# Pooled attention, expert layer and slot experts on one core: the last quarter of w2 reordered early, second-layer sums per column half, and the last token rows written by pairs

## The chip, the cores and the metric

The kernel is one program on one core of a Trainium2 chip. The core has a matrix engine (PE, whose weight loads stand apart as PEld), a vector engine (DVE), a scalar engine (ACT), GpSimd (POOL) and a sync engine (SP). SP issues every DMA of this kernel; 16 DMA engines carry them out. The metric is the device time of one execution in microseconds. The engines run their own instructions in order and wait for each other through semaphores.

## The reference

Three stages follow each other, on 4608 tokens (36 tiles of 128) and 512 columns, all in float32:

```
k_p, v_p = mean of k, v over 8 neighbouring positions
x   = softmax(q k_p^T / sqrt(64)) v_p          # 8 batches x 8 heads, as 4608 x 512
x   = relu(x @ w_in)^2 @ w_out                 # 512 -> 2048 -> 512
logits = x @ phi                               # 4608 x 32 slots
d   = softmax of logits over the tokens;  slot_input = d^T @ x       # 32 slots x 512
slot_out[e] = relu(slot_input[e] @ w1[e]) @ w2[e]     # 8 experts, 4 slots each, 512 -> 1024 -> 512
c   = softmax of logits over the 32 slots
out = c @ slot_out                             # 4608 x 512
```

The change touches only the end of this: the product with w2 (8 x 1024 x 512, 16.8 MB), the last line, and when a quarter of w2 is read.

## The kernel before, in words

Up to about 680 us a table of slots (`ev`, filled by `at`, run by `run_slot`) drives a loop over token tiles: attention of a tile, its product with w_in (L492, the bulk of the matrix work), squares, logits, and running sums over the tokens. The squared tiles `g` go to DRAM (`g_dram`, L532) and come back turned. The keys and values (`kv`, L147) and the queries (`qt`, L130, in 16 or more small pieces) are loaded through SP between these stores. A scheduler places the instructions; SP works through its DMAs in order, over eight semaphores, so that a DMA is issued only after the one eight places before it has landed.

Then comes the tail. `project` makes the slot inputs. `first(r, n, kks)` is the first expert layer for experts 4r to 4r+3 and half n of the hidden columns, four experts side by side in 32 columns of the PE array each; `turn_h` turns its result. Between `turn_h(0, 1)` and `first(1, 1)` five transposes (`slot_turn`, L783) turn the slot weights c of the token groups 4 to 8 (a group is four token tiles), and `slot_out` copies them back.

`second` (through `queued`, so its instructions have line L1228) adds one chunk of 128 hidden rows of the second layer. The kernel before first sums all eight chunks of experts 0 to 3 and the first four chunks (fc 0 to 3) of experts 4 to 7, 512 columns wide, into one PSUM bank `misc`; ACT copies it to `slot_part`. `slots_of(h)` then does one half h of the columns: the last four chunks (fc 4 to 7) of experts 4 to 7 at 256 columns into `po`, DVE adds `slot_part` (L1295), PE spreads the sum over the four 32-row groups (`pr`, L1297), ACT copies it to `slots` (L1298). The weights for these last chunks are read by `load_w2(h, 1, 1)`, eight DMAs of 512 KB (L872) in runs of 256 columns, 1 KB.

`combine(h, ss, n)` makes the output of the token groups 2n and 2n+1 for one half of the columns: eight matmuls with 32 rows (one 32-row group of the array for each u) and 128 columns, then two copies on DVE and two on ACT, and four stores of 256 KB in 1 KB runs (L1325). It runs for h = 0, then `slots_of(1)`, then for h = 1. `combine_rows(g)` does the groups 4 to 8 over all 512 columns: four matmuls of 32 rows by 128 columns (L1334) into four banks, four copies, four stores of 256 KB, 2 KB a row (L1345). The matmul results lie in six PSUM banks (`l1`, `gT`, `att`, two each); `l`, `gT` and `att` in the rows below are these.

Of the kernel before, what the change touches and what calls it, by code (L numbers as in the profile page):

```python
# [17 lines left out]
def kernel(  # L18
# [21 lines left out]
    P = 128  # L40
# [44 lines left out]
    wo_dram = dram.tile([P, DFF // P, DM], F32, tag="wo_dram", name="wo_dram")  # L85
    g_dram = [dram.tile([2, NQ, CPQ, P, P], F32, tag=f"g_dram{t}", name=f"g_dram{t}") for t in range(0, NT - 4, 2)]
# [767 lines left out]
    def load_w2(h, r, fg):  # L854
# [15 lines left out]
        for i in range(4):  # L870
            fc = 4 * fg + i
            w2t["last"] = nc.sync.dma_start(  # L872
                out=parts[i],
                in_=w2[4 * r:4 * r + 4, fc * P:(fc + 1) * P, h * HD:(h + 1) * HD].rearrange("e p d -> p e d"),
            )
            w2t[h, r, fc] = [parts[i][:, j] for j in range(4)]

# [96 lines left out]
    for j in range(PC, NQ):  # L974
        for kk in range(KD):
            at(CS[j - 2][kk], paced, conv_in, j, kk)
    at(0, load_w, "in", 2)
# [290 lines left out]
    queued(slot_turn, 4, 8)  # L1268
    behind(["siT"], slot_out, 4, 8, nc.vector.tensor_copy)
    queued(slot_turn, 8, 9)  # L1270
    slot_out(8, 9, nc.scalar.copy)
# [17 lines left out]
    def slots_of(h):  # L1289
        po = ps1.tile([P, HD], F32, tag="pl", name="po")  # L1290
        for fc in range(NFC // 2, NFC):
            second(po, NR - 1, fc, w2t[h, NR - 1, fc], fc == NFC // 2, fc == NFC - 1)
        so = slot_part[:, h]
        ss = slots[:, h]
        nc.vector.tensor_tensor(out=so, in0=po, in1=so, op=ALU.add)  # L1295
        pr = ps1.tile([P, HD], F32, tag="pl", name="pr")
        mark[f"pr{h}"] = nc.tensor.matmul(pr, s4rep.rearrange("p a b -> p (a b)"), so)  # L1297
        nc.scalar.copy(out=ss, in_=pr)  # L1298
        return ss
# [3 lines left out]
    def combine(h, ss, n):  # L1303
# [6 lines left out]
        for a, g in enumerate(groups):  # L1310
            for u in range(4):
                b = slice(32 * u, 32 * u + 32)
                with ExitStack() as es:
                    if (a, u) != (0, 0):
                        es.enter_context(tc.issue_after(mark["row"].ins))
                    mark["row"] = nc.tensor.matmul(banks[u][:, a * HD:(a + 1) * HD], lt_sb[b, 4 * g:4 * g + 4].rearrange("p u s -> p (u s)"), ss[b])
# [10 lines left out]
    def combine_rows(g):  # L1327
        banks = []
        for u in range(4):
            banks.append(ps(tags[n_out[0] % 3]))  # L1330
            n_out[0] += 1
        for u in range(4):
            b = slice(32 * u, 32 * u + 32)
            mark["row"] = nc.tensor.matmul(  # L1334
                banks[u],
                lt_sb[b, 4 * g:4 * g + 4].rearrange("p u s -> p (u s)"),
                slots[b].rearrange("p h d -> p (h d)"),
            )
        for u in range(4):
            o = gp.tile([P, DM], F32, tag="g", name="o")  # L1340
            if u % 2:
                nc.scalar.copy(out=o, in_=banks[u])
            else:
                nc.vector.tensor_copy(o, banks[u])
            nc.sync.dma_start(out=out[(4 * g + u) * P:(4 * g + u + 1) * P], in_=o)  # L1345

    po = psm()
    chunks = [(0, fc) for fc in range(NFC)] + [(NR - 1, fc) for fc in range(NFC // 2)]
    for r, fc in chunks:
        if (r, fc) == (0, NFC // 2):  # L1350
            turn_h(1, 0)
            turn_h(1, 1)
        second(po, r, fc, w2t[r, fc], (r, fc) == chunks[0], (r, fc) == chunks[-1])
    slot_part = p2.tile([P, 2, HD], F32, tag="r", name="slot_part")
    nc.scalar.copy(out=slot_part.rearrange("p h d -> p (h d)"), in_=po)
    ss0 = slots_of(0)
    with tc.issue_after(w2t["last"].ins):
        for n in range(2):
            combine(0, ss0, n)
    ss1 = behind(["row"], slots_of, 1)  # L1360
    for n in range(2):
        combine(1, ss1, n)
    for g in range(4, NT // 4):
# [31 lines left out]
```

## Time and profile before

| | us |
|---|---|
| three runs, median (lowest to highest) | 754.03 (751.69 to 756.07) |
| the profiled execution | 751.86 |
| its span in the trace | 750.1 |
| PE busy in the span | 715.6 |
| DVE busy | 524.3 |
| ACT busy | 387.8 |

The profiled execution lasted 1.8 us longer than its span, and it was 2.2 us faster than the median of the runs. Times in the rows below are microseconds from the start of the span. A matmul in float32 stands as two instructions in the trace, so that 16 matmuls of the program are "x32" there. A busy PE is one that has a matmul in flight, which says nothing on how well the array is filled.

### The profile page before, as it was taken

To read this page: it belongs to the slowest core of one execution; us is meant where nothing else is said; L and a number is where in the kernel's file an instruction comes from. 1 tells how busy PE (TensorE), PEld (TensorE's weight loads), DVE (VectorE), ACT (ScalarE), POOL (GpSimd) and SP (SyncE) were. 2 spreads that over 40 slices of the span, in tenths; PEclk is the share of its full clock that TensorE was granted. 3 is DMA by queue.
4 is the path that set the end of the run, shared out by engine and by line. 5 is a ranking of instruction groups with operands and counts; after the bars stand their busy time and mean duration, and the time that the engine had idled before them with its cause. 6 is when DMAs were issued, how large, how long until landed. Compare 5 with 4: busy or idle time off the path is not lost.

```text
span 750.1 us, 13911 instructions
## 1 busy us (share of the span) xinstructions
PE 715.6 (95%) x4969; PEld 497.4 (66%) x4969; DVE 524.3 (70%) x1048; ACT 387.8 (52%) x1132; POOL 136.5 (18%) x151
## 2 busy tenths in 40 slices
PE   7799899999999999999999999999999999999985
PEld 7677678787776767666666656667666766764342
DVE  4998854497896788878979787778878574414132
ACT  3766767464656456346646462637466453333132
POOL 2234400004971400050342120320000000000000
PEclk9999999999999999999999999999999999999996
DMA  8967945658776996686998788879676434988998
GB/s 256 257 198 237 260 136 155 218 144 258 213 224 163 274 258 185 191 251 169 250 283 232 195 242 241 229 204 262 181 231 213 141 127 147 410 326 341 394 303 337
DMA packets 213012, 175.05 MB, mean 233 GB/s; under 512 B 75216, under 2 KB 169424, under 8 KB 212944
## 3 DMA queue, kind: packets, MB, share of 16 engines
q1 hardware_dynamic: 212944, 174.17, 75.7%
q8 instruction: 39, 0.64, 0.3%
q14 instruction: 29, 0.24, 0.1%
HBM read 126.94 MB, written 47.19 MB: 232 GB/s over the span
## 4 chain that ended last, share of the span: by engine, by line
PE 56%; DVE 19%; DMA 9%; ACT 6%; issue 5%; POOL 3%; SPq 1%; POOLq 0%; DVEq 0%; ACTq 0%
PE l L492 33%; PE misc L743 3%; ACT es L258 2%; DMA kv<-in_v_dram 2%; POOL w L429 2%; PE pl L616 2%; ACT aT L306 2%; DVE es L287 2%; DVE aT L308 2%; PE l L1228 2%; PE att L340 2%; DMA kv<-in_k_dram 2%; PE gT L340 2%; DMA tmp<-g_dram 1%; PE misc L1228 1%
## 5 line engine op out<-in xcount | busy, mean ns | idle before, releaser
L492 PE MATMUL l<-w,xh 128*128 128x512 f32 x1152 | 380.0, 409 | 4.4 <-DVE tmp L528 1.6
L492 PEld LDWEIGHTS l<-w,xh 128*128 128x128 f32 x1152 | 207.8, 189 | 70.3 <-issue 16.9
L492 PE MATMUL l<-w,xl 128*128 128x512 f32 x576 | 229.5, 400 | 0.3 <-DVE xl L351 0.3
L520 ACT ACTIVATE r<-l 128x512 f32<-128x512 f32 x142 | 85.6, 604 | 153.4 <-PE l L492 145.4
L492 PEld LDWEIGHTS l<-w,xl 128*128 128x128 f32 x576 | 108.4, 188 | 29.5 <-issue 4.2
L154 POOL TENSOR_TENSOR kv<-kv 72x512 f32<-72x512 f32 x40 | 53.9, 1350 | 221.5 <-DMA kv<-in_v_dram 115.2
L306 ACT COPY aT<-turned 32x256 f32<-32x256 f32 (+1 forms) x168 | 67.8, 404 | 25.5 <-DVE turned L328 22.7
L258 ACT ACTIVATE es<-att,mx 128x72 f32<-128x72 f32 x120 | 37.1, 336 | 24.1 <-DVE mx L253 23.7
L528 DVE TENSOR_TENSOR g<-l,r 128x512 f32<-128x512 f32 x55 | 37.5, 682 | 17.0 <-ACT r L520 10.8
L580 DVE STREAM_TRANSPOSE turned<-turned 128x1024 f32<-128x1024 f32 x39 | 47.5, 1229 | 1.9 <-DMA turned<-g_dram 1.8
L258 ACT ACTIVATE es<-gT,mx 128x72 f32<-128x72 f32 x120 | 36.7, 330 | 9.8 <-DVE mx L253 9.8
L308 DVE COPY aT<-turned 32x256 f32<-32x256 f32 (+1 forms) x120 | 40.5, 337 | 1.7
L429 POOL TENSOR_TENSOR w<-tmp,w 128x512 fp32r<-128x512 f32 x16 | 28.4, 1780 | 61.9 <-ACT w L427 53.2
L530 ACT ACTIVATE g<-r 128x512 f32<-128x512 f32 x54 | 34.4, 639 | 0.7
L528 DVE TENSOR_TENSOR tmp<-l,r 128x512 f32<-128x512 f32 x33 | 22.6, 684 | 17.1 <-ACT r L520 14.4
L287 DVE TENSOR_TENSOR es<-es,rs 128x576 f32<-128x576 f32 x36 | 33.3, 927 | 0.9
L580 DVE STREAM_TRANSPOSE tmp<-tmp 128x1024 f32<-128x1024 f32 x25 | 30.3, 1224 | 5.2 <-DMA tmp<-g_dram 5.2
L155 POOL TENSOR_TENSOR kv<-kv 72x256 f32<-72x256 f32 x40 | 33.6, 848 | 0.9
L374 ACT ACTIVATE tmp<-st 128x512 f32<-128x512 f32 x32 | 21.5, 676 | 14.9 <-DMA st<-in_moe_w_in_dram 10.0
L376 DVE TENSOR_SCALAR tmp<-tmp 128x512 uint32<-128x512 uint32 x32 | 15.5, 485 | 16.3 <-ACT tmp L374 16.3
L743 PE MATMUL misc<-g,d 128*32 128x512 f32 x134 | 25.7, 629 | 1.2 <-DVE d L730 0.7
L385 DVE SCALAR_TENSOR_TENSOR tmp<-st,tmp 128x512 f32<-128x512 uint32 x32 | 26.3, 824 | 0.6
(232 smaller groups left out, 1060.2 us busy)
## 6 DMA issues: line engine op xcount, KB each, us to landing
g_dram<-g SPq DMA_DIRECT2D x95, 256.0 KB
w<-in_moe_w_dram SPq DMA_DIRECT2D x44, 512.0 KB
turned<-g_dram SPq DMA_DIRECT2D x39, 512.0 KB
tmp<-g_dram SPq DMA_DIRECT2D x25, 512.0 KB
g_back<-g_dram SPq DMA_DIRECT2D x40, 256.0 KB
kv<-in_k_dram SPq DMA_DIRECT2D x32, 288.0 KB
kv<-in_v_dram SPq DMA_DIRECT2D x32, 288.0 KB
out_dram<-o SPq DMA_DIRECT2D x36, 256.0 KB
```

The lines of the kernel that those rows point to most:

```text
L154: eng.tensor_tensor(out=x[:, :, 0:4], in0=x[:, :, 0:4], in1=x[:, :, 4:8], op=ALU.add)
L258: mark["es", t] = nc.scalar.activation(out=es[:, e], in_=sv[:, h], func=AF.Exp, bias=mx[:, e:e + 1], accum_out=rsum[:, t % 8, e, 0:1],)
L287: mark["norm", t] = nc.vector.tensor_tensor(out=es, in0=es, in1=rs.unsqueeze(2).to_broadcast([P, H, SP]), op=ALU.mult)
L306: nc.scalar.copy(out=dst, in_=src)
L308: eng[e].tensor_copy(dst, src)
L429: nc.gpsimd.tensor_tensor(out=w[kk][:, 1], in0=c, in1=w[kk][:, 0].bitcast(F32), op=ALU.subtract)
L492: mm = mark["l1", t, j] = nc.tensor.matmul(hp, steps[i][0], steps[i][1], start=(i == 0), stop=(i == n - 1))
L520: nc.scalar.activation(out=r, in_=hp, func=AF.Relu, scale=1.0 / (R * R if sq == "V" else R))
L528: mark["sq"] = nc.vector.tensor_tensor(out=dst, in0=pre, in1=src, op=ALU.mult)
L530: nc.scalar.activation(out=dst, in_=src, func=AF.Square)
L580: nc.vector.transpose(out=gc.rearrange("p (n i) -> p n i", i=32), in_=gc.rearrange("p (n f) -> p n f", f=32))
L743: mark["dg"] = nc.tensor.matmul(dp[32 * j:32 * j + 32], d[:, u], g if t < NT - 4 else natural(g), start=(u == 0), stop=(u == width(t) - 1),)
```

## The change

1. A DRAM tile `w2h` is added. Sixteen new DMAs (`split_w2`) copy the last quarter of w2 (experts 4 to 7, fc 4 to 7, 4.2 MB) from its place in w2 into `w2h`, DRAM to DRAM, in 1 KB runs; they are placed at the slots 29, 31, ... 59, each right after the latest store of `g`. The late loads of these weights then read `w2h`, where a partition's 1024 numbers (four experts, 256 columns) lie together: 4 KB runs.
2. The 512-wide sum in `misc` now ends with experts 0 to 3. Experts 4 to 7 are summed per column half over all eight chunks (`half_of`), fc 0 to 3 from 256-column slices of the same tiles. The second half's chunks 0 and 1 stand between the first half's sum and its spreading matmul, chunk 2 behind that, chunk 3 between the two `combine` calls of the first half, chunks 4 to 7 after them.
3. The five transposes of the slot weights of the groups 4 to 8, and their copies, move from before `first(1, 1)` to behind the first half's `combine` calls.
4. The groups 4 to 8 are written by pairs of neighbouring tokens: the weights of a matmul are 64 columns, every second token of a tile; two token tiles fill one bank per parity, the upper and lower 64 partitions. One store then carries two token tiles, 512 KB, with 4 KB for each partition. Forty matmuls of 32 rows by 64 columns stand for twenty of 32 by 128; ten stores for twenty. Their SBUF tiles `o` come from the pool `wp` and no longer from `gp`.

```
+    w2h = dram.tile([2, NFC // 2, P, 4, DM // 2], F32, tag="w2h", name="w2h")
...
-                in_=w2[4 * r:4 * r + 4, fc * P:(fc + 1) * P, h * HD:(h + 1) * HD].rearrange("e p d -> p e d"),
+                in_=w2h[h, i],
...
+    def split_w2(h, i, e):
+        fc = NFC // 2 + i
+        nc.sync.dma_start(
+            out=w2h[h, i, :, e:e + 2],
+            in_=w2[4 * (NR - 1) + e:4 * (NR - 1) + e + 2, fc * P:(fc + 1) * P, h * HD:(h + 1) * HD].rearrange("e p d -> p e d"),
+        )
...
+    for n in range(16):
+        at(29 + 2 * n, pinned, "store", split_w2, n // 8, n // 2 % 4, n % 2 * 2)
...
     turn_h(0, 1)
-    queued(slot_turn, 4, 8)
-    behind(["siT"], slot_out, 4, 8, nc.vector.tensor_copy)
-    queued(slot_turn, 8, 9)
-    slot_out(8, 9, nc.scalar.copy)
     first(1, 1, range(KD))
...
-    def slots_of(h):
-        po = ps1.tile([P, HD], F32, tag="pl", name="po")
-        for fc in range(NFC // 2, NFC):
-            second(po, NR - 1, fc, w2t[h, NR - 1, fc], fc == NFC // 2, fc == NFC - 1)
...
+    def half_of(h, fcs):
+        if h not in po_t:
+            po_t[h] = psm()[:, :HD] if h else ps1.tile([P, HD], F32, tag="pl", name="po")
+        for fc in fcs:
+            if fc < NFC // 2:
+                w = [x[:, h * HD:(h + 1) * HD] for x in w2t[NR - 1, fc]]
+            else:
+                w = w2t[h, NR - 1, fc]
+            second(po_t[h], NR - 1, fc, w, fc == 0, fc == NFC - 1)
+        if fcs[-1] == NFC - 1:
+            so = slot_part[:, h]
+            mark["so"] = nc.vector.tensor_tensor(out=so, in0=po_t[h], in1=so, op=ALU.add)
+
+    def spread(h):
+        pr = psm()[:, :HD] if h else ps1.tile([P, HD], F32, tag="pl", name="pr")
+        queued(nc.tensor.matmul, pr, s4rep.rearrange("p a b -> p (a b)"), slot_part[:, h])
+        nc.scalar.copy(out=slots[:, h], in_=pr)
...
-    def combine_rows(g):
...
+    pairs = lt_sb.rearrange("p (g u) s -> p g (u s)", u=4).rearrange("p g (m e) -> p g e m", e=2)
+
+    def combine_rows(n):
+        o = wp.tile([P, 2, DM], F32, tag="w", name="o")
...
+        for e in range(2):
+            for x in range(2):
+                u = 2 * (n % 2) + x
+                b = slice(32 * u, 32 * u + 32)
+                queued(
+                    nc.tensor.matmul,
+                    banks[e][64 * x:64 * x + 64],
+                    pairs[b, n // 2, e],
+                    slots[b].rearrange("p h d -> p (h d)"),
+                )
+        for e in range(2):
+            (nc.scalar.copy if e else nc.vector.tensor_copy)(out=o[:, e], in_=banks[e])
+        nc.sync.dma_start(
+            out=out[2 * P * n:2 * P * (n + 1)].rearrange("(p e) d -> p (e d)", e=2),
+            in_=o.rearrange("p e d -> p (e d)"),
+        )
...
+    half_of(0, range(NFC))
+    half_of(1, [0, 1])
+    spread(0)
+    half_of(1, [2])
+    with tc.issue_after(w2t["last"].ins):
+        combine(0, 0)
+        half_of(1, [3])
+        combine(0, 1)
+    with tc.issue_after(mark["so"].ins):
+        queued(slot_turn, 4, 8)
+        slot_out(4, 8, nc.vector.tensor_copy)
+        queued(slot_turn, 8, 9)
+        slot_out(8, 9, nc.scalar.copy)
+    half_of(1, range(NFC // 2, NFC))
+    spread(1)
     with tc.issue_after(w2t["last"].ins):
         for n in range(2):
-            combine(0, ss0, n)
...
+            combine(1, n)
+        for n in range(8, NT // 2):
+            combine_rows(n)
```

PE, from the sums of experts 4 to 7 to the first output matmul, before (`w_10` and `w_11` hold the chunks fc 0 to 3 of these experts, `w_011` the fc 4 to 7 of column half 0):

```order
L1228 MATMUL misc<-w_10_7259,hT 32x512 x8
L1228 MATMUL misc<-w_11_7264,hT 32x512 x8
L1228 MATMUL po<-w_011_7269,hT 32x256 x4
L1228 MATMUL po<-w_011_7270,hT 32x256 x4
L1228 MATMUL po<-w_011_7271,hT 32x256 x4
L1228 MATMUL po<-w_011_7272,hT 32x256 x4
L1297 MATMUL pr<-slot_part,s4rep 128x256
L1316 MATMUL l_7547<-slots,lt_sb 128x256
```

The same place now; here `misc` is the sum of column half 1:

```order
L1238 MATMUL po<-w_10_7276,hT 32x256 x8
L1238 MATMUL po<-w_11_7281,hT 32x256 x8
L1238 MATMUL po<-w_011_7286,hT 32x256 x4
L1238 MATMUL po<-w_011_7287,hT 32x256 x4
L1238 MATMUL po<-w_011_7288,hT 32x256 x4
L1238 MATMUL po<-w_011_7289,hT 32x256 x4
L1238 MATMUL misc<-w_10_7276,hT 32x256 x8
L1238 MATMUL pr<-slot_part,s4rep 128x256
L1238 MATMUL misc<-w_11_7281,hT 32x256 x4
L1238 MATMUL l_7568<-slots,lt_sb 128x256
```

The sixteen 512-column matmuls became sixteen of 256 columns for half 0, and those of half 1 moved behind its sum, around the spreading matmul.

PE again, from the last output matmul of half 0 to the first of half 1, before (`w_111` holds fc 4 to 7 of half 1):

```order
L1316 MATMUL l_7573<-slots,lt_sb 128x256
L1316 MATMUL gT<-slots,lt_sb 128x256
L1228 MATMUL po<-w_111_7277,hT 32x256 x16
L1297 MATMUL pr<-slot_part,s4rep 128x256
L1316 MATMUL att<-slots,lt_sb 128x256
```

The same place now:

```order
L1238 MATMUL l_7598<-slots,lt_sb 128x256
L1238 MATMUL gT<-slots,lt_sb 128x256
L784 MATMUL att<-ident,lt_sb 128x128 x5
L1238 MATMUL misc<-w_111_7294,hT 32x256 x16
L1238 MATMUL misc<-slot_part,s4rep 128x256
L1238 MATMUL att<-slots,lt_sb 128x256
```

The five transposes stand ahead of the second half's last sums, and write two `att` banks.

SP, in the stretch in which the keys of the fourth batch are loaded, before:

```order
L130 DMA qt<-in_q_dram 32x2x32
L147 DMA kv<-in_k_dram 72x2x512
L532 DMA g_dram_106<-g 128x4x128
L147 DMA kv<-in_k_dram 72x2x512 x2
L407 DMA st<-in_moe_w_out_dram 128x1024 x3
L532 DMA g_dram_106<-g 128x4x128
L407 DMA st<-in_moe_w_out_dram 128x1024
```

The same stretch now, with the last two of the sixteen copies:

```order
L533 DMA g_dram_107<-g 128x4x128
L881 DMA w2h<-in_moe_w_dram 128x2x256
L131 DMA qt<-in_q_dram 32x2x32
L131 DMA qt<-in_q_dram 32x6x32
L131 DMA qt<-in_q_dram 32x2x32
L148 DMA kv<-in_k_dram 72x2x512 x2
L408 DMA st<-in_moe_w_out_dram 128x1024 x2
L533 DMA g_dram_107<-g 128x4x128
L881 DMA w2h<-in_moe_w_dram 128x2x256
L408 DMA st<-in_moe_w_out_dram 128x1024 x2
```

Each copy stands behind a store of `g` and ahead of queries, keys or w_out pieces, which SP now issues after it.

## Rows read from the trace of the kernel before

**Rows 1.** The page's DMA line: busy tenths in 40 slices of the span.
```profile
DMA  8967945658776996686998788879676434988998
```

**Rows 2.** Windows of the tail: busy us and instructions per engine, PEclk, DMA share, GB/s.
```profile
695.00:700.00 5.00, 5.00 (x49) 2.40 (x45) 1.00 (x2) 1.35 (x2) 0.00 (x0) 1.00 1.03 418
716.00:717.00 1.00, 0.83 (x16) 0.26 (x8) 0.03 (x1) 0.00 (x0) 0.00 (x0) 1.00 1.10 349
719.00:720.00 1.00, 1.00 (x20) 0.72 (x12) 0.23 (x1) 0.19 (x1) 0.00 (x0) 1.00 0.81 256
720.00:721.00 1.00, 0.65 (x10) 0.47 (x10) 1.00 (x2) 0.89 (x2) 0.00 (x0) 1.00 0.10 33
723.00:724.00 1.00, 0.51 (x12) 0.03 (x4) 0.42 (x1) 0.00 (x0) 0.00 (x0) 1.00 0.37 120
726.00:727.00 1.00, 0.78 (x12) 0.36 (x4) 0.62 (x2) 0.57 (x2) 0.00 (x0) 1.00 1.03 340
740.00:745.00 5.00, 1.05 (x3) 0.00 (x0) 1.39 (x2) 1.33 (x3) 0.00 (x0) 0.50 0.99 384
748.00:749.00 1.00, 0.00 (x0) 0.00 (x0) 0.00 (x0) 0.00 (x0) 0.00 (x0) 0.50 0.19 72
```

**Rows 3.** SP's timeline in the tail: start, us from first to last issue, DMA, count.
```profile
700.86 12.99 SPq L872 DMA_DIRECT2D w<-in_moe_w_dram  x8
720.49 11.87 SPq L1325 DMA_DIRECT2D out_dram<-o  x16
```

**Rows 4.** PE's timeline in the tail: start, us, line, tile, array rows*columns, shape.
```profile
699.27 0.71 PE L783 MATMUL att<-ident,lt_sb 128*128 128x128 f32 x5
...
711.49 3.62 PE L1228 MATMUL misc<-w,hT 128*32 128x512 f32 x32
714.92 1.91 PE L1228 MATMUL po<-w,hT 128*32 128x256 f32 x32
...
718.61 0.48 PE L1316 MATMUL l<-slots,lt_sb 32*128 32x256 f32 x1 [0.46 <-ACT slots L1298]
...
718.62 0.48 PE L1316 MATMUL att<-slots,lt_sb 32*128 32x256 f32 x1
...
720.52 0.48 PE L1316 MATMUL l<-slots,lt_sb 32*128 32x256 f32 x1 [0.35 <-DVE o L1323]
...
721.58 1.93 PE L1228 MATMUL po<-w,hT 128*32 128x256 f32 x32
...
725.22 0.48 PE L1316 MATMUL att<-slots,lt_sb 32*128 32x256 f32 x1 [0.46 <-ACT slots L1298]
...
727.73 0.69 PE L1334 MATMUL gT<-slots,lt_sb 32*128 32x512 f32 x1
727.73 0.69 PE L1334 MATMUL att<-slots,lt_sb 32*128 32x512 f32 x1
...
728.70 0.69 PE L1334 MATMUL l<-slots,lt_sb 32*128 32x512 f32 x1
```

**Rows 5.** DVE's timeline in the tail.
```profile
716.97 0.42 DVE L1295 TENSOR_TENSOR slot_part<-po,slot_part 128x256 f32<-128x256 f32 x1 [7.98 <-PE po L1228]
719.77 0.69 DVE L1323 COPY o<-l 128x512 f32<-128x512 f32 x1 [2.38 <-PE l L1316]
```

**Rows 6.** Windows of the stretch in which the sixteen copies are placed.
```profile
100.00:125.00 25.00, 25.00 (x136) 19.97 (x136) 16.37 (x33) 18.28 (x59) 0.00 (x0) 1.00 0.44 123
125.00:150.00 25.00, 24.91 (x255) 19.32 (x251) 11.91 (x25) 12.57 (x25) 0.00 (x0) 1.00 0.63 199
150.00:175.00 25.00, 25.00 (x160) 20.52 (x158) 21.75 (x49) 16.11 (x54) 0.00 (x0) 1.00 0.51 139
```

**Rows 7.** One store of 256 KB: issue on SP, ns shortest/median/longest.
```profile
L1325 SPq DMA_DIRECT2D out_dram<-o x16: 372/450/1657, 720.5 to 731.7; - x16
```

**Rows 8.** POOL's last pooling of the fourth batch's keys, and their use on PE.
```profile
195.52 0.90 POOL L156 TENSOR_TENSOR kp<-kv 72x128 f32<-72x128 f32 x1
...
211.81 0.45 PE L203 MATMUL att<-ident,kp 72*128 72x72 f32 x4
```

More of the change, by code (lines that the diff above doesn't have):

```diff
@@ L1287, in second, with combine @@
             )
-    def slots_of(h):
-        po = ps1.tile([P, HD], F32, tag="pl", name="po")
-        for fc in range(NFC // 2, NFC):
-            second(po, NR - 1, fc, w2t[h, NR - 1, fc], fc == NFC // 2, fc == NFC - 1)
[L1293 to L1299, printed above, removed]
+    po_t = {}
+    def half_of(h, fcs):
[14 more added lines that the diff above has]
+        nc.scalar.copy(out=slots[:, h], in_=pr)
     n_out = [0]
-    def combine(h, ss, n):
+    def combine(h, n):
         groups = range(2 * n, min(2 * n + 2, NT // 4))
@@ L1312, in combine @@
                 b = slice(32 * u, 32 * u + 32)
[L1313 to L1316, printed above, removed]
+                queued(
+                    nc.tensor.matmul,
+                    banks[u][:, a * HD:(a + 1) * HD],
+                    lt_sb[b, 4 * g:4 * g + 4].rearrange("p u s -> p (u s)"),
+                    slots[b, h],
+                )
         for u in range(4):
@@ L1325, in combine @@
             nc.sync.dma_start(out=rows[u, :, 2 * n:2 * n + w, h * HD:(h + 1) * HD], in_=o)
-    def combine_rows(g):
+    pairs = lt_sb.rearrange("p (g u) s -> p g (u s)", u=4).rearrange("p g (m e) -> p g e m", e=2)
+    def combine_rows(n):
+        o = wp.tile([P, 2, DM], F32, tag="w", name="o")
         banks = []
-        for u in range(4):
+        for e in range(2):
             banks.append(ps(tags[n_out[0] % 3]))
             n_out[0] += 1
[L1332 to L1345, printed above, removed]
+        for e in range(2):
+            for x in range(2):
+                u = 2 * (n % 2) + x
+                b = slice(32 * u, 32 * u + 32)
+                queued(
+                    nc.tensor.matmul,
+                    banks[e][64 * x:64 * x + 64],
+                    pairs[b, n // 2, e],
+                    slots[b].rearrange("p h d -> p (h d)"),
+                )
+        for e in range(2):
+            (nc.scalar.copy if e else nc.vector.tensor_copy)(out=o[:, e], in_=banks[e])
+        nc.sync.dma_start(
+            out=out[2 * P * n:2 * P * (n + 1)].rearrange("(p e) d -> p (e d)", e=2),
+            in_=o.rearrange("p e d -> p (e d)"),
+        )
@@ L1347 @@
     po = psm()
-    chunks = [(0, fc) for fc in range(NFC)] + [(NR - 1, fc) for fc in range(NFC // 2)]
-    for r, fc in chunks:
-        if (r, fc) == (0, NFC // 2):
+    for fc in range(NFC):
+        if fc == NFC // 2:
             turn_h(1, 0)
             turn_h(1, 1)
-        second(po, r, fc, w2t[r, fc], (r, fc) == chunks[0], (r, fc) == chunks[-1])
+        second(po, 0, fc, w2t[0, fc], fc == 0, fc == NFC - 1)
     slot_part = p2.tile([P, 2, HD], F32, tag="r", name="slot_part")
     nc.scalar.copy(out=slot_part.rearrange("p h d -> p (h d)"), in_=po)
-    ss0 = slots_of(0)
+    half_of(0, range(NFC))
@@ L1360 @@
[L1360 to L1363, printed above, removed]
-        combine_rows(g)
+            combine(1, n)
+        for n in range(8, NT // 2):
+            combine_rows(n)
 _INS = ["q", "k", "v", "moe_w_in", "moe_w_out", "moe2_phi", "moe2_w1", "moe2_w2"]
```

## The prediction

> **What bounds the kernel now.** I read the page's slices first, then windows over the tail, then the timelines of SP, PE and DVE there, and last the stretch in which the new copies are placed. In the slices the DMA line stands at 8 or 9 in the last six digits, from about 640 us on [rows 1]. Before that the transfers lie under the matrix work: from 100 to 175 us PE has a matmul in flight in 74.9 of 75 us, with the DMA engines at 0.44, 0.63 and 0.51 [rows 6].
>
> The tail is a bound of transfers with one hole in it. The last weights are loaded without a pause (share 1.03 to 1.10), first at 418 GB/s, then, in the eight pieces with 1 KB runs, at 349 GB/s; the share is 0.81 from 719 to 720 us and 0.10 in the next [rows 2], so I put the end of the loads at 719.8. The first store is issued at 720.49 [rows 3]. It waits for a chain on PE: the sums of experts 4 to 7 from 711.49, the last of them from 714.92, DVE's addition at 716.97, the output matmuls at 718.61 and the copy at 719.77 [rows 4, 5]. From 724 us on the stores fill the engines again, 340 GB/s in 1 KB runs and 384 GB/s in 2 KB runs, until 748.2 (share 0.19 from 748 to 749) [rows 2]. So three things set the end: when the loads are through, when the first store can start, and how fast 9.4 MB of output go out.
>
> **The change part by part.** The sum is made against the profiled execution, 751.86 us, which is 2.2 us under the median of the runs, 754.03.
>
> *Transposes moved.* Five transposes of 0.71 us go from PE's path [rows 4]; the next matmuls overlap their end a little, I take 0.65.
>
> *Sums per half.* Before, 7.1 us lie between 711.49 and 718.61: 3.4 for four chunks at 512 columns, 1.9 for four chunks at 256 columns, and 1.8 for the addition, spreading matmul and copy [rows 4, 5]. Now half 0 needs eight chunks at 256 columns, 2 x 1.9 = 3.8. The spreading matmul stands behind two chunks of half 1, a quarter of 3.8 or 0.95, where before it waited about 0.6 for the addition, so the last piece becomes 2.1. That is 5.9 instead of 7.1, a gain of 1.2. With the transposes the output matmuls start 1.85 earlier, at 716.8, and the first store, 1.9 behind them as before, at 718.65.
>
> *Loads.* The eight pieces are 4.19 MB: 12.0 us at 349 GB/s, 10.1 at 418, the rate of the pieces before them, which have 4 KB rows [rows 2]. The loads end at 717.9 instead of 719.8. Each piece is there before its sum: half 0 needs its last piece at about 714, and at 1.26 us a piece from 707.8 on (719.8 less the 12.0) it is through at 712.8. The hole between loads and stores therefore keeps its length, 1.6 us with the 0.9 from issue to data that I take, and moves 1.9 earlier.
>
> *First half's stores.* Eight stores, 2.1 MB at 340 GB/s, last 6.2 us: from 719.5 to 725.7.
>
> *Second half.* Before, half 1 starts its output at 725.22 [rows 4]. Now PE goes from 716.8: the second `combine` waits 1.9 for a bank as it did (718.61 to 720.52), runs 1.1 with its matmuls (720.52 to 721.58) [rows 4], then 0.7 of transposes, 1.9 for the last four chunks, and 1.7 for addition, spreading and copy: 724.1. I add 0.2, because the fifth transpose writes an `att` bank that a copy of the second `combine` must empty first: 724.3, a gain of 0.9. Behind it stand DVE's and ACT's copies of half 1 and no other work, so this wait costs only what it leaves empty on the DMA engines: half 1's data start at 724.3 + 1.9 + 0.9 = 727.1, when half 0's stores have been through for 1.4 us. That is a new hole. The one before at 723 to 724, with a share of 0.37 [rows 2], stands beside an issue of 1.66 us where the median is 0.45 [rows 7]; I let it fall into the new hole. Half 1's stores end at 727.1 + 6.2 = 733.3.
>
> *Rows by pairs.* 5.24 MB of output go out in 4 KB runs. No row shows such a store. The near bound is 384 GB/s, the 2 KB stores [rows 2], 13.65 us, no change; the far bound is 418, the 4 KB loads, 12.5 us. Stores in 1 KB runs stand at 340 beside loads at 349, so I take 405, near the loads: 12.9. Copies stay two of about 0.7 us for each 512 KB, on two engines, under the 1.3 that the transfer takes. Their tiles are no longer reused inside this stage, so no copy waits for a store. The stores end at 746.2 instead of 748.2, a gain of 2.0.
>
> *PE in that stage.* There are 40 matmuls where 20 stood. What one costs beside its neighbours is not in the trace: bounds follow from rows. Four row groups that write four banks start together (718.61 and 718.62), and a pair of 512-column matmuls takes 0.97 us (727.73 to 728.70) [rows 4]. If the two tiles of a bank run together, and the next pair of row groups beside them, one store's four matmuls take about 0.97 us; if all are serial, 3.9. I take 0.97, because in the sums four tiles side by side in the columns already write one bank together (32 instructions in 3.6 us, where at 0.48 each, half of the 0.97, they would take 15 one after the other). At that pace PE is through at 737, and the stores, which reach these rows at 733.3, never wait.
>
> *The sixteen copies.* A DRAM to DRAM transfer is not in the trace. Between the 1 KB stores (340 GB/s) and a load and a store one after the other, 256 KB take 0.77 to 1.5 us, all sixteen 12 to 25 us of the DMA engines. Their cover is 100 to 175 us, where these are idle for about half of 75 us [rows 6]. On SP each costs some 0.45 us of issue [rows 7], 7 us in all, ahead of query pieces, kv loads and g stores. The four last stand ahead of the keys of the fourth batch, whose pooling ends at 196.4 and which PE takes at 211.81 [rows 8], 15 us later. I cost them at 0; if the cover fails, the late keys cost PE what exceeds those 15 us, and a late query tile some 2 to 6 us. A gain is excluded there, since PE had no idle time to give back.
>
> Sum: 2.0 off the end; the 1.9 from the last data to the end of the span stays. The profiled execution becomes 749.8, and the median 754.0 - 2.0 = 752.0.
>
> **Rivals.**
>
> *PE becomes the bound of the last rows.* If the two row groups that write one bank exclude each other, the first of a pair still overlaps with the second matmul of the group before, so a store's four matmuls take two times 0.97, 1.95 us, against 1.3 for its transfer. Ten of them from 727 on end at 746.5; copy, issue and the last transfer add 3.0, and data end at 749.5, 1.3 later than now: 755.3, slower. It decides once a store's matmuls need more than about 1.7 us, since PE has a lead of 6 us. For it speaks that no row shows two row groups in one bank; against it, that the column tiles share one without loss. [...]
>
> *The copies are not hidden.* A query tile or the values of a batch come late behind copies and stores in SP's order, PE stops, and nothing later gives it back. Four copies at 1.5 us and 0.45 of issue are 7.8 us; if 5 or 6 of them reach PE, the median is 757.5. Against it stand the full PE windows and the half-idle DMA engines [rows 6] and the 15 us of [rows 8].
>
> *The new hole closes.* If the first half's stores still suffer a long issue, or half 1 comes with no added 0.2, and the 4 KB stores reach 418 GB/s, the end comes 3.5 to 4.5 us earlier: 750.
>
> *The stores do not care for 4 KB runs* and the hole of 1.4 is whole: a gain of 1.2, 752.8. I count this with the forecast.
>
> **How the numbers follow.** A measurement here cannot tell less than 0.5%, 3.8 us, from no change. Forecast, with its own range of 750.3 to 753.5: 0.66. New hole closed, 750: 0.14. PE as bound, 755.3: 0.12. Copies not hidden, 757.5: 0.08. The three runs of before lie 4.4 us apart, so a median can be off by 1.3 either way; with that, 752.0 comes out below 750.3 about once in six. Faster by over 0.5%: 0.66/6 + half of 0.14, and a little for a 4 KB store that is quicker than any row, 0.23. Slower by over 0.5% (above 757.8): half of the copies' case and a little of PE's, 0.08. Within: 0.69. The range goes to 748.8 below, for the closed hole, and to 755.6 above, so that it holds PE's case and leaves out most of the copies'.
>
> **What would show it.** Right: loads at over 410 GB/s to their end at about 718; first store issued near 718.7; half 1's output matmuls near 724.3, with the DMA share low for about a us before its stores; last stores at 395 GB/s or more; the tail before 700 us at the same times as now. Wrong: matmuls of the last rows that reach beyond 740 us, with copies waiting for PE (PE as bound); idle PE between 100 and 220 us, or a later start of the tail (copies); no gap behind half 0's stores (hole closed). A tail as forecast beside an unchanged total would mean that the time was lost before 700 us, and that my cover for the copies was wrong.

## The result: slower by half a per cent, and the profile after

The changed kernel takes 755.79 us in the median of 22 runs, the kernel before 752.59 on the same chip: a ratio of 1.0051 with an interval of 1.0035 to 1.0068. The forecast was 752.0 and a gain. The profiled execution has a span of 753.8 us where before had 750.1.

Where the 3.7 us of the spans lie is read from one matmul that stands in both kernels at the head of the tail. PE's timeline, before and then after (columns: start, length, engine, line, operation, tiles, how many; in brackets the idle time ahead of it and what ended it):

```profile
682.92 1.29 PE L1197 MATMUL misc<-wot,accT 128*32 128x256 f32 x20
```

```profile
687.54 1.29 PE L1207 MATMUL misc<-wot,accT 128*32 128x256 f32 x20
...
719.34 0.64 PE L1238 MATMUL po<-w,hT 128*32 128x256 f32 x8 [0.58 <-DMA w<-w2h]
...
721.99 0.48 PE L1238 MATMUL l<-slots,lt_sb 32*128 32x256 f32 x1
```

The tail starts 4.62 us late, and from there on the changed kernel needs 66.3 us to its end where before needed 67.2. So the tail gained 0.9 us, and 4.6 were lost ahead of it. They were not lost where the copies stand. Windows of after (window, its length, then busy us of PE, PEld, DVE, ACT, POOL with their instructions, granted clock, DMA share, GB/s), with the first three to be laid beside [rows 6]:

```profile
100.00:125.00 25.00, 25.00 (x134) 20.21 (x132) 16.36 (x32) 18.25 (x59) 0.00 (x0) 1.00 0.53 139
125.00:150.00 25.00, 24.74 (x255) 19.08 (x254) 11.74 (x24) 13.11 (x26) 0.00 (x0) 1.00 0.89 284
150.00:175.00 25.00, 25.00 (x161) 20.79 (x160) 21.77 (x48) 15.49 (x52) 0.00 (x0) 1.00 0.62 174
225.00:250.00 25.00, 22.09 (x148) 16.13 (x147) 12.19 (x20) 12.36 (x26) 9.80 (x12) 1.00 0.81 220
240.00:245.00 5.00, 2.40 (x43) 1.37 (x41) 3.67 (x8) 0.76 (x2) 1.32 (x1) 1.00 1.03 278
```

Beside the copies PE stays full, though the DMA share rises from 0.63 to 0.89. The hole comes 65 us later: from 240 to 245 us PE works 2.40 us of 5. In the kernel before the last two windows read:

```profile
225.00:250.00 25.00, 24.14 (x162) 18.25 (x161) 14.88 (x25) 13.15 (x27) 3.61 (x7) 1.00 0.70 199
240.00:245.00 5.00, 5.00 (x57) 3.88 (x57) 2.42 (x3) 1.27 (x3) 1.30 (x3) 1.00 0.63 156
```

What the hole costs is read from PE's matmuls on its two sides. A matmul of L492 that starts at 238.51 us in before starts at 238.76 in after (L493 there), 0.25 us late; behind the hole (before, then after):

```profile
244.66 0.97 PE L467 MATMUL misc<-s,at_sb 128*128 128x32 f32 x8
```

```profile
247.85 0.98 PE L468 MATMUL misc<-s,at_sb 128*128 128x32 f32 x8
```

That is 3.19 us late, so 2.9 of the 4.6 us go in the hole. Another 1.1 go near 280 us, where PE waits once more, 0.68 us for DVE (windows of before, then after):

```profile
270.00:290.00 20.00, 20.00 (x140) 13.78 (x139) 16.36 (x34) 7.86 (x28) 0.00 (x0) 1.00 0.81 231
```

```profile
270.00:290.00 20.00, 19.19 (x139) 13.12 (x138) 16.04 (x32) 8.87 (x28) 0.00 (x0) 1.00 0.82 246
```

The rest, 0.25 us before 238 us and 0.3 between 290 us and the tail, is small.

In the windows from 225 us on, the number to look at is POOL's: 9.80 us of pooling from 225 to 250 us where there were 3.61. POOL is late. Followed back from the hole, PE waits for DVE and DVE for a reload of the squared tiles (after):

```profile
241.22 1.25 DVE L581 STREAM_TRANSPOSE turned<-turned 128x1024 f32<-128x1024 f32 x1 [7.44 <-DMA turned<-g_dram]
...
242.52 0.64 PE L617 MATMUL pl<-turned,a_sb 128*32 128x256 f32 x8 [2.10 <-DVE turned L581]
```

SP issues that reload behind value, key and query loads. Its timeline in before, then in after:

```profile
214.27 0.43 SPq L147 DMA_DIRECT2D kv<-in_v_dram  x1
...
222.02 6.00 SPq L130 DMA_DIRECT2D qt<-in_q_dram  x12
...
229.51 0.51 SPq L572 DMA_DIRECT2D turned<-g_dram  x1
```

```profile
221.59 0.33 SPq L148 DMA_DIRECT2D kv<-in_v_dram  x1
...
227.85 8.48 SPq L131 DMA_DIRECT2D qt<-in_q_dram  x12
...
236.88 0.51 SPq L573 DMA_DIRECT2D turned<-g_dram  x1
```

The value load is 7.3 us late and so is the reload. What held SP's queue is POOL, which had not yet freed the `kv` tiles. The queue's waits from 170 to 300 us, of before and then of after (engine, line, what it waited for: us in total, times, longest):

```profile
SPq L147 <- POOL vp L156: 5.9, 3, 2.8
SPq L147 <- POOL kp L156: 5.8, 3, 3.2
```

```profile
SPq L148 <- POOL vp L157: 9.1, 4, 5.1
...
SPq L148 <- POOL kp L157: 7.0, 3, 6.1
```

SP waited for POOL in before too, but never for more than 3.2 us at a time.

In the tail itself SP's rows answer to [rows 3] (late loads, stores of the halves, stores by pairs):

```profile
705.53 8.99 SPq L873 DMA_DIRECT2D w<-w2h  x8
...
723.87 13.53 SPq L1341 DMA_DIRECT2D out_dram<-o  x16
737.50 10.44 SPq L1363 DMA_DIRECT2D out_dram<-o  x10
```

and the windows to [rows 2]:

```profile
714.00:715.00 1.00, 1.00 (x16) 0.26 (x8) 0.00 (x0) 0.00 (x0) 0.00 (x0) 1.00 1.02 410
...
722.00:723.00 1.00, 1.00 (x20) 0.71 (x16) 0.00 (x0) 0.00 (x0) 0.00 (x0) 1.00 0.43 168
...
750.00:751.00 1.00, 0.00 (x0) 0.00 (x0) 0.00 (x0) 0.00 (x0) 0.00 (x0) 0.50 1.02 418
751.00:752.00 1.00, 0.00 (x0) 0.00 (x0) 0.00 (x0) 0.00 (x0) 0.00 (x0) 0.50 0.22 86
```

Less 4.62, the loads end near 717.9 (forecast 717.9), the output matmuls start at 717.4 (716.8), the first store at 719.25 (718.65). The last stores run at 418 GB/s.

### The profile page after: what moved, and what is told of

It is laid out like the page before. It is cut to its first block, busy times and chain, and to the rows that moved or that the text cites. A ratio compares the mean times of both kernels' runs of the same rounds, so it can differ in the third digit from the quotient of the medians.

```text
span 753.8 us, 14050 instructions
## 1 busy us (share of the span) xinstructions
PE 714.4 (95%) x5041; PEld 498.4 (66%) x5041; DVE 522.6 (69%) x1048; ACT 386.7 (51%) x1132; POOL 135.5 (18%) x151
## 4 chain that ended last, share of the span: by engine, by line
PE 60%; DVE 12%; DMA 12%; issue 5%; ACT 4%; POOL 2%; SPq 2%; POOLq 0%; DVEq 0%; ACTq 0%
PE l L493 38%; DMA turned<-g_dram 3%; PE misc L744 3%; PE pl L617 3%; DMA w<-in_moe_w_dram 2%; POOL w L430 2%; PE att L341 2%; PE gT L246 2%; ACT aT L307 2%; PE gT L341 2%; DMA kv<-in_v_dram 2%; DVE es L288 2%; PE att L246 2%; DMA w<-w2h 1%; PE att L617 1%
## 5 line engine op out<-in xcount | busy, mean ns | idle before, releaser
L493 PE MATMUL l<-w,xh 128*128 128x512 f32 x1152 | 381.1, 410 | 7.8 <-DVE tmp L529 3.3
L493 PEld LDWEIGHTS l<-w,xh 128*128 128x128 f32 x1152 | 208.4, 189 | 73.9 <-issue 17.1
L493 PE MATMUL l<-w,xl 128*128 128x512 f32 x576 | 230.1, 401 | 0.3 <-DVE xl L352 0.3
L493 PEld LDWEIGHTS l<-w,xl 128*128 128x128 f32 x576 | 108.7, 189 | 29.6 <-issue 4.2
L309 DVE COPY aT<-turned 32x256 f32<-32x256 f32 (+1 forms) x120 | 40.1, 335 | 1.6
L259 ACT ACTIVATION_READ_ACCUMULATOR es<-att,mx 128x1 f32 x120 | 26.2, 219 | 0.0
```

The lines of the kernel that those rows point to most:

```text
L259: mark["es", t] = nc.scalar.activation(out=es[:, e], in_=sv[:, h], func=AF.Exp, bias=mx[:, e:e + 1], accum_out=rsum[:, t % 8, e, 0:1],)
L309: eng[e].tensor_copy(dst, src)
L493: mm = mark["l1", t, j] = nc.tensor.matmul(hp, steps[i][0], steps[i][1], start=(i == 0), stop=(i == n - 1))
```

## The experiments

The first question is why POOL is late. The copies do two things: they take room and time on SP's queue and on the DMA engines, and they make the scheduler place other instructions otherwise. Up to the tail PE, DVE and ACT have the same order in both kernels; on SP the keys and values of the fourth batch move behind copies, query pieces and stores, and on POOL seven pooling operations change places. Theory A1 says that this order is the loss, rival B that the bytes are, A2 that the issues are; rival D blames the new tail.

**e1, no copies.** `for n in range(16): at(29 + 2 * n, ..., split_w2, ...)` is taken out, and `in_=w2h[h, i]` is again the slice of w2.

> The changed kernel without its sixteen copies: the eight late pieces of w2 are read straight from w2 in 1 KB runs, as before; the new combination of the tail stays. Theory A (the copies cost about 4.6 us between 240 and 285 us, and the new tail gains 0.9 to 1.6 us): PE follows the kernel before to within 0.5 us up to 680 us, no DVE wait of over 2 us for turned<-g_dram there, and the time is 0.1 to 0.3% under before, 750.5 to 751.8 us. Rival D (the new tail is what loses, the lag at 240 to 285 us is chance): still 0.3 to 0.5% over before, 755 to 756 us.

1.001 [0.9985, 1.0035], 752.09 us beside 751.57. PE busy from 225 to 250 us: 24.80. D falls; but the gain that A gave to the new tail does not show either. (In its profile PE has another hole, at 276 us, and the clock falls to 0.54 for 3 us behind it; at this place its PE loses 3.3 us with no copy in the kernel, so the 1.1 us that after lost near 280 us are not shown to come from the copies.)

**e2, copies only.** The kernel before with `split_w2`, its sixteen places and `in_=w2h[h, i]`.

> The kernel before with only the sixteen copies and the eight late loads from the copied array; halves, pairs and slot weights as before. Theory A: the lag of 4 to 5 us stands at 285 us as in the changed kernel, the loads end 1.9 us earlier in the tail and bring at most 0.7 us, so 0.5 to 0.6% over before, 756 to 757.5 us. Rival D: no lag, 752 to 753 us.

1.0078 [1.0047, 1.0109]. The hole is there without the new tail, and here the clock falls behind it; two windows of e2:

```profile
240.00:243.00 3.00, 0.93 (x10) 0.16 (x8) 1.85 (x4) 0.69 (x2) 0.00 (x0) 1.00 1.06 317
243.00:250.00 7.00, 6.50 (x46) 5.40 (x43) 4.30 (x8) 0.59 (x1) 3.25 (x5) 0.51 0.79 216
```

After 2.1 idle us PE runs at a granted clock of 0.51 for 7 us, which costs some 3 us more. In the profile of after the same hole kept the clock at 1.00. From 238 to 250 us PE falls 2.9 us behind before in after and 5.7 in e2: what the hole cost in these two differs with the clock behind it.

**e3, tiny copies.**

```
-            out=w2h[h, i, :, e:e + 2],
+            out=w2h[h, i, :2, e:e + 2],
```

with two rows of w2 as source, and the late loads from w2.

> The changed kernel with its sixteen copies cut to 2 of the 128 partitions each (4 KB instead of 256 KB) in the same places of SP's order, with the order of every other instruction as in the changed kernel; the eight late pieces are read straight from w2. What it parts is order and issue from bytes. Theory A1 (the order: the key and value loads of the fourth batch stand 10 to 30 places later on SP and POOL's pooling comes in another order): the lag at 285 us stays, 3 to 5 us, 755 to 756.5 us. Rival B (the 4.2 MB that the copies write and the 4.2 MB they read delay the other transfers): the lag is gone, as without copies, 750.5 to 752 us.

1.0089 [1.0065, 1.0114], 757.12 us: B falls. Without the bytes nothing is better. The hole has moved to 228 to 233 us, though, and looks different (timelines of e3, three engines):

```profile
225.48 4.43 DVE L309 COPY aT<-turned 32x256 f32<-32x256 f32 x5
...
226.47 1.29 POOL L155 TENSOR_TENSOR kv<-kv 72x512 f32<-72x512 f32 x1 [0.34 <-DMA kv<-in_k_dram]
...
229.86 0.66 PE L452 MATMUL gT<-ident,st 128*128 128x128 f32 x4 [1.90 <-ACT wt L454]
232.85 1.22 PE L493 MATMUL l<-w,xh 128*128 128x512 f32 x2 [2.34 <-DVE g L529]
```

Five small copies on DVE take 4.43 us (the same five 1.47 in after), beside additions of the late POOL; what stands behind them on DVE is late, and PE stops; behind the hole its clock is at 0.50 for 5 us.

**e4, sixteen copies closer together.** `at(29 + n, ...)` in place of `at(29 + 2 * n, ...)`. POOL's order is now that of before.

> The changed kernel with the same sixteen copies at slots 29 to 44 (one each) instead of 29 to 59 (every second): the same bytes and issues in the same stretch, but POOL's order and the order of the key and value loads on SP stay as before. Theory A1 (the order): the lag at 285 us is under 1 us, the tail keeps its gain, 750.5 to 751.8 us, 0.1 to 0.3% under before. Rival B (bytes) and rival A2 (sixteen more issues in SP's queue by themselves): the lag of 3 to 5 us stays, 755 to 756.5 us.

1.0026 [1.0002, 1.0049]. No hole at 240 us (24.34 busy from 225 to 250). There is one of its own: a copy in almost every place of SP's queue puts a key load behind them, and PE waits at 143.07 us (e4), after which the granted clock is 0.50 until 149 us:

```profile
143.07 2.19 PE L162 MATMUL att<-ident,kv 72*64 72x72 f32 x32 [2.31 <-DMA kv<-in_k_dram]
```

So crowding costs something by itself, in the medians less than the four kernels with a moved order lose.

**e5 and e6, a pair that differs in one digit.** Eight copies of 512 KB, four slots apart and three slots apart:

```
+    for n in range(8):
+        at(29 + 4 * n, pinned, "store", split_w2, n // 4, n % 4)
```

This is e5; e6 has `29 + 3 * n`. Four apart, POOL and SP have a moved order again: seven pooling operations stand in other places than in before, though not quite in those of after. Three apart, both have the order of before.

> The changed kernel with eight copies of 512 KB at the slots 29, 33, ... 57 in place of sixteen of 256 KB at 29, 31, ... 59: the same bytes, half the issues. With this spacing the value and key loads on SP and the pooling on POOL still stand in the changed kernel's order. Theory A1 (the order costs): the hole of some 2.5 us between 240 and 245 us stays, 755 to 757 us. Rival A2 (the number of issues in SP's queue costs): half of the loss or less, 752 to 753.5 us.

> The same eight copies of 512 KB at the slots 29, 32, ... 50, three apart and not four. POOL's order and the order of all other DMAs on SP are now those of the kernel before. Theory A1: no PE hole of over 1 us between 225 and 245 us, the tail's gain of 0.9 us remains, 750.5 to 752 us. Rival B (bytes or issues cost, wherever their order): as with four apart, 755 to 757 us.

e5: 1.0085 [1.0051, 1.0118]. e6: 0.9998 [0.9966, 1.003]. The same bytes and the same issues, and 0.9% between them. The window of e5, then that of e6:

```profile
225.00:245.00 20.00, 16.24 (x77) 12.23 (x79) 12.63 (x22) 11.55 (x35) 7.51 (x8) 0.83 0.72 200
```

```profile
225.00:245.00 20.00, 19.01 (x134) 13.75 (x133) 12.58 (x24) 13.73 (x33) 5.44 (x9) 1.00 0.62 168
```

PE is 2.8 us short in e5, and its clock stands at 0.83. This settles it against B and A2, since the bytes and the number of issues are the same. A1 is left, with one reservation: in every kernel with a moved order (after, e2, e3, e5) some copies stand in the slots 51 to 59, and in no kernel with the order of before. No run has the one without the other, so the order is shown as the cause only together with these places.

**e7 and e8, other places for the sixteen.** `at(226 + 2 * n, ...)` and `at(20 + 2 * n, ...)`; both keep POOL's order.

> The changed kernel with its sixteen copies at the slots 226 to 256, in the stretch from about 575 to 640 us where the DMA share of the kernel before is 0.41 to 0.69; POOL's order and that of the other DMAs up to there as before. Theory A1: PE follows the kernel before up to 575 us, the copies lie beside half-idle DMA engines and SP has few loads to hold up, 750.5 to 752 us. Rival (copies cost wherever they stand, since they push w1's loads or the last g stores back by 0.56 us of issue each): a hole between 575 and 700 us, 753 to 757 us.

> The changed kernel with its sixteen copies at the slots 20 to 50, two apart as in the changed kernel but nine slots earlier, so that the order of POOL and of SP's other DMAs stays as before. Theory A1: no hole at 240 us, 750.5 to 752 us. Rival B: a loss as in the changed kernel, 755 to 756 us. The stretch from 75 to 100 us already had a DMA share of 0.85, so a new hole before 100 us is possible; it would show as PE idle there and add what it lasts.

e7: 1.0002 [0.9973, 1.003]. e8: 0.9967 [0.9937, 0.9998], the only version whose whole interval lies under before. **e16** repeats e8:

> The changed kernel with its sixteen copies at the slots 20 to 50 once more, against the kernel before on the same chip. If the ratio of 0.9967 was the tail's gain of 0.9 us beside an undisturbed order: 0.997 to 1.000 again, about 0.999. If it was chance: up to 1.002.

0.9987 [0.9961, 1.0013]. The two intervals overlap, so the better figure may be partly chance; e8 is the best version, by 0.1 to 0.3%, and the second interval includes no gain. **e10**, eight copies at `20 + 4 * n`:

> The changed kernel with eight copies of 512 KB at the slots 20, 24, ... 48; the order of all other DMAs and of POOL is exactly that of the kernel before. Theory A1 (the order costs, and neither bytes nor issues): as with sixteen copies from slot 20 on, 0.2 to 0.4% under before, 749.5 to 751 us, no hole between 225 and 245 us. Rival B: 753 us or more.

1.0001 [0.9981, 1.0021]: no harm, and no gain, against what I expected.

All these on one table, PE busy from 225 to 250 us and the granted clock there:

| kernel | order on POOL | PE busy of 25 | clock | ratio to before |
|---|---|---|---|---|
| before | as before | 24.14 | 1.00 | 1 |
| after | moved | 22.09 | 1.00 | 1.0051 |
| e2 | moved | 22.27 | 0.86 | 1.0078 |
| e3 | moved | 20.76 | 0.86 | 1.0089 |
| e5 | moved | 21.24 | 0.86 | 1.0085 |
| e1, e4, e6, e7, e8, e10 | as before | 24.01 to 25.00 | 1.00 | 0.9967 to 1.0026 |

**e9, POOL work beside DVE's copies.** Is the slow DVE of e3 the cause by itself? The kernel before, with (`spare` is set up elsewhere)

```
+        if t == min(EX):
+            scr = spare[0][:SP]
+            for _ in range(6):
+                nc.gpsimd.tensor_tensor(out=scr, in0=blk[:SP, :, 0], in1=blk[:SP, :, 1], op=ALU.add)
```

> The kernel before with six additions of 72x256 on POOL that read what DVE's first five turned copies of the attention weights read (at 224.5 us in the kernel before, 1.74 us for the five); nothing else is moved but one piece of the queries by one place. Theory P (DVE's small copies slow down while POOL runs an addition, so that pooling that comes late does harm even where nothing waits for it): the five copies take 3.5 to 4.5 us, PE has a hole of 1 us or more between 226 and 233 us, 0.2 to 0.7% over before, 753 to 757 us. Rival (the long copies in the slow kernels have another cause, and POOL's own work costs DVE nothing): the copies stay at 1.4 to 1.8 us, no hole, 751 to 752.5 us.

0.9985 [0.9962, 1.0007]. Timelines of e9:

```profile
223.75 3.24 DVE L312 COPY aT<-turned 32x256 f32<-32x256 f32 x5
...
224.44 5.23 POOL L302 TENSOR_TENSOR turned<-turned 72x256 f32<-72x256 f32 x6
...
228.93 0.74 PE L496 MATMUL l<-w,xh 128*128 128x512 f32 x2 [0.41 <-DVE g L532]
```

DVE does slow down, from 1.74 us to 3.24, but PE's wait is 0.41 us. Theory P is half right: the copies do slow down, but the 1.5 us are hidden, and behind them PE is no later than before (L496 at 228.93 us, the same matmul at 229.11 in before). In e3 the slow copies added 2.7 to 3.0 us at a place where pooling was late as well. How the loss divides between the late reload and the slow copies stays open: after and e2 show the first, e3 the second (e5's copies took 3.78 us), and the total is alike.

The second question is the tail. **e12** is the kernel before with rows by pairs alone, **e11** is e8 with each of these stores split by parity into two of 256 KB with 2 KB runs.

> The kernel before with only the rows of the groups 4 to 8 written by pairs; no copies, no sums per half, transposes in their old place. Theory: the store stage of these rows is 1.1 us shorter (418 against 384 GB/s over 5.24 MB), 0.7 us of that is given back at the end by one late DMA engine, so from PE's last hidden tile at 667 us to the end of the span 0.3 to 0.5 us less than before, 751 to 752.3 us. Rival (the whole gain of the tail is the pairs): 0.9 us less.

> The kernel with sixteen copies from slot 20 on, with each store of the last rows split by parity into two of 256 KB in 2 KB runs, twenty in place of ten; matmuls and copies as in the changed kernel. If the 4 KB runs are what lifts these stores from 384 to 420 GB/s: the last stores fall back to 380 to 390 GB/s, data end 1.0 to 1.3 us later, but the last 0.7 us in which one of the 16 engines works alone goes, so the span is 0.2 to 0.5 us longer than with 4 KB. If the rate comes from the pairs alone (fewer, larger stores): no change of rate for half-size stores with 2 KB runs either, 418 GB/s.

e12: 0.999 [0.9969, 1.0011], and from its first store (717.09) to its end (747.7) it takes 30.6 us where before took 29.6. The pairs alone make the store stage longer; in e12's last 1.6 us the DMA engines move 22 to 30 GB/s. e11: 1.0006 [0.9985, 1.0026]; its last stores run at about 405 GB/s, between the 384 of before and the 420 of 4 KB, so neither of its two cases holds, and one engine is still late (24 GB/s at the end). What that is stands in the DMA view of after from 731 to 753 us (40 slices of 0.55 us: GB/s; then the queues with packets, MB, share):

```profile
GB/s 4 0 289 330 356 344 328 332 374 311 335 289 166 384 419 426 406 432 402 439 402 439 402 432 410 425 424 425 417 417 425 417 425 410 425 417 276 22 22 0
...
q8 instruction: 1, 0.02, 0.3%
```

At the end the rate falls to 22 GB/s, about what one engine of sixteen moves (418/16 is 26), for 1.2 us. And there is a fetch of 16 KB of instructions, 0.3% of 16 engines' 22 us, about 1 us of one engine. Before has none in its last 22 us:

```profile
GB/s 350 343 345 335 358 345 335 356 341 339 332 352 341 372 384 376 395 372 372 384 376 410 361 384 391 372 399 369 391 372 387 384 372 391 369 395 376 384 205 0
...
q14 instruction: 1, 0.01, 0.1%
```

Theory F: the change has 72 more matmuls and 72 more weight loads on PE (5041 of each for 4969), so PE's fortieth fetch now falls into the stores (at 735.8 us, 1.7 ahead of the first store by pairs), and the engine that carries it cannot catch up at full load. **e13** moves the fetch in e8, **e14** does the same to before as a control:

```
-        for _ in range(11):
-            nc.tensor.matmul(warm, ident, ident)
+        for _ in range(39):
+            nc.tensor.matmul(warm[:24, :24], ident[:, :24], ident[:, :24])
```

> The kernel with sixteen copies from slot 20 on, with the 11 warming matmuls of 128x128 at the start of PE replaced by 39 of 24x24: 112 more entries in PE's list of instructions ahead of everything else, about the same start. In all profiles with rows by pairs a fetch of 16 KB of instructions (queue q8, 0.93 us of one DMA engine) falls into the last stores, and one engine ends 1.2 to 1.3 us behind the others; in the kernel before there is none. [...] Rival G (4 KB runs or pairs of themselves leave one engine late): 1.2 us as before.

> The kernel before, with the same 39 small warming matmuls for the 11: a control with 112 more instructions of PE and the old rows. Theory F: its next fetch of 16 KB now falls into the last stores (some 57 instructions of PE before the end), where there was none, and one engine is late at the end by up to 0.9 us, less what it catches up, since 2 KB stores leave its engines 3 to 4% idle; from the end of the bulk to the end of the span 2 to 3 us. Rival G: no late engine, 1.9 us. Both: 751 to 753 us.

The time got worse, 1.0025 [0.9998, 1.0053] and 1.0092 [1.0055, 1.0129], which I had not expected. In both profiles the clock stands at half from about 13 to 30 us (granted 0.55 and 0.56 from 12 to 31 us, 0.91 in before). But e7, with the eleven large matmuls, has it at 0.8 and 0.7 in the first two of the page's 40 slices, where before has 0.9 in both, so the profiles do not show that the small matmuls bring this; why the medians are worse stays open. The end answers the question of the fetch. e13, DMA view from 730 to 752 us:

```profile
GB/s 348 84 24 197 348 346 341 326 352 343 324 346 348 343 404 439 387 439 402 425 402 432 410 432 402 432 410 424 410 424 439 395 454 380 462 380 454 127 0 0
...
q14 instruction: 1, 0.01, 0.1%
```

No 16 KB fetch, and no slices at 22: the engines end together. From first store to end e13 takes 29.2 us (723.59 to 752.8), e8 30.4 (719.24 to 749.65). F holds: with the fetch ahead of 730 us, where e13's view begins, and so before the hole between the halves' stores, no engine is late at the end; in the hole one is (84 and 24 GB/s in the view above, in after 4 and 0), while the next stores are still to come. e14, DMA view from 730 to 752 us:

```profile
GB/s 145 277 320 345 331 196 346 341 332 358 345 345 352 398 376 387 376 380 384 384 380 384 387 387 384 376 391 372 387 384 369 395 380 387 376 380 384 302 19 0
q8 instruction: 1, 0.02, 0.3%
```

The fetch stands there just before 731 us, at the start of half 1's stores, ahead of the last rows, and the rate of 19 lasts for less than one slice of 0.55 us. So with the old rows at about 384 GB/s the delay was nearly made up. Whether the slower stores or the longer time did that is not parted, and a fetch among the last rows themselves, which e14 was to bring, was not tried.

**e15**: e8 with the 11 warming matmuls kept and 28 of 8x8 behind them.

> The kernel with sixteen copies from slot 20 on, with the 11 warming matmuls of 128x128 kept and 28 of 8x8 put behind them: 112 more entries in PE's list, without the clock at half for 17 us at the start that the replaced warming brought in the run before. Theory F: the 16 KB fetch leaves the last stores, the engines end within 0.5 us of each other, the start is 0 to 2 us later (PE has idle time at 11 to 14 and 20 to 22 us to take it up), 750 to 752 us. If the extra matmuls at the start are not taken up: 752 to 754 us.

1.0014 [0.9993, 1.0035]; first store to end 29.1 us (720.08 to 749.2), so the 1.2 us are there again, and the median, 753.19, shows nothing of them. The start does not explain that: at 106 us e15's profile is 1.2 us behind before, but e8's, without the 28 matmuls, 1.7. It stays open; 1.2 us are 0.16%, less than the interval.

## Why the prediction was wrong

*The sixteen copies, cost 0: the step that failed.* I wrote that their cover is the stretch from 100 to 175 us, and that the four last stand ahead of keys which PE takes 15 us after their pooling. PE was indeed full there. But the step counted issues and bytes, and asked which engine takes the moved loads next. It did not ask what else the moved loads hold. Late value and key loads make POOL late; POOL then holds the `kv` tiles that SP must fill next, SP's queue stands still for 5 to 6 us at a time, and a reload that has nothing to do with keys comes 7.4 us late, 45 us after the last slack that I had looked at, and costs PE 2.9 us in the profile of after and 5.7 in that of e2. Between 175 us and the tail I had read no rows of any engine but those of [rows 8]. With the order of before, eight or sixteen copies cost nothing that the medians show (e6, e7, e8, e10), and crowded ones little (e4): the 0 was right for bytes and issues, and the order was the price. Which part of it (late pooling, slow copies on DVE, the clock) takes how much stays open. The rival "copies not hidden" had the place, SP's order, and a price of 757.5 that e2, e3 and e5 come close to; I gave it 0.08. The base hid part of the miss: I took 754.03, the median of three runs, and 22 runs of the same kernel give 752.59. A gain of 2.0 from there would be 750.6, so 5.2 us lie between the forecast change and the 755.79 measured.

*The tail, 2.0 us.* It gained 0.9 in the span. Output matmuls: 1.85 forecast, 1.24 measured (34.45 us from the head of the tail for 35.69). The missing 0.6 is the wait of 0.58 in the row at 719.34: "each piece is there before its sum, at 712.8" was wrong. The piece came at 714.7, by after's clock 719.3; I had used the mean rate of all 16 engines; why the piece came later than that was not tried by itself. In e8 there are two such waits, 1.3 us together. Store stage: forecast 29.45 us from first store to end (718.65 to 748.1), measured 29.9 (723.87 to 753.8). The rate was better than forecast (418 for 405), and the late engine's 1.2 us, for which the sum had no term, took more than that back.

*Right:* loads at 410 GB/s; the new hole of about 1 us ahead of half 1's stores (4 and 0 GB/s in the view from 731 us); and PE is not the bound of the last rows. After's PE timeline:

```profile
733.70 0.59 PE L1238 MATMUL att<-slots,lt_sb 32*64 32x512 f32 x2
733.77 0.59 PE L1238 MATMUL gT<-slots,lt_sb 32*64 32x512 f32 x2
734.12 0.59 PE L1238 MATMUL att<-slots,lt_sb 32*64 32x512 f32 x2
```

Two tiles of one bank, from different row groups and in different halves of its partitions, start together (x2), and the next two 0.07 us after them; two such pairs start every 0.43 us. The rival's condition was that two row groups that write one bank exclude each other. Here the two wrote one at the same time, 0.59 us each, and neither waited for the other.

*In sum:* 4.6 us lost ahead of the tail, 2.9 of them at 240 us and 1.1 near 280, against 0.9 gained. That the tail's gain does not stand out in the medians with the order kept (0.9967 to 1.0026 over six kernels) is no contradiction: 0.9 us is 0.12%, less than these intervals. It also means that no median shows the gain; it is read from profiles alone.

## What to carry to other kernels

When instructions are added to a queue that works in order, compare the order of everything else before and after, and price what moved, not only what was added; a load that moves behind others is paid where its buffer is next needed, perhaps two batches later. Try the same addition a few slots away: if the order can be kept, work that cost half a per cent may cost nothing that can be measured. And this tail, at 418 GB/s, had no room for one engine's extra 1.2 us: count instructions there as well as bytes.

## What was not expected of the hardware

DVE's small copies were mostly slower while POOL added. In after the copies of L309 (ns shortest/median/longest) take

```profile
L309 DVE COPY aT<-turned x120: 237/283/1379, 224.1 to 621.2; 32x256 f32<-32x256 f32 x72, 8x256 f32<-8x256 f32 x48
```

Worked out copy by copy, the 105 with little or no POOL work beside them last 0.24 to 0.29 us; the other 15 last 0.73 on average, and the longest, 1.38, about as long as one pooling addition (1.29). Three of the 15 are not slowed. What slowed the other twelve was not shown.

A fetch of 16 KB of instructions took about 1 us of one DMA engine (0.3% of 16 engines' 22 us in the view of after from 731 us). Before has 39 such fetches on queue q8, after 40. The trace does not name the engine that they are for; I take them for PE's, since the 10,082 matmuls and weight loads of after, over 40 fetches, are 252 for each, and the 9938 of before, over 39, are 255. In after, whose last stores run at 418 GB/s, the delay stays to the end; in e14, with the old rows at about 384 GB/s and the fetch at the start of half 1's stores, little of it was left.

A hole of 2 to 3 us in PE's work cost as much again in clock in e2 (0.51 over 7 us) and nothing in after (1.00).
